# Chunked attention with two mixtures of experts, one core: v in rows interleaved by head, k copied by POOL, k and q in one transfer

## The chip, the core and the metric

The kernel runs as one program on one core of one Trainium2 chip. The core has five engines with an instruction queue each: PE (matrix multiply, with PEld for its weight loads), DVE and ACT (elementwise work and reductions), POOL (the same) and SP, which here issues the transfers between HBM and SBUF. Sixteen DMA engines carry the transfers out. SBUF has 128 partitions (rows). The metric is the device time of one execution in microseconds; three runs of the kernel before took 248.13, 250.2 and 254.1 us, the median is 250.2.

## What is computed

Attention in chunks of 32 queries: each chunk sees 8 memory rows, 16 rows to its left, its own 32 and 8 to its right. A soft mixture of experts and then a top-1 mixture follow on the 3072 tokens of 512 features.

```python
q, k, v: (4, 8, 768, 64);  mem_k, mem_v: (4, 8, 8, 64)
for c in range(24):
    k_ctx = k[:, :, max(0, 32*c - 16) : min(768, 32*c + 40)]      # v_ctx likewise
    k_full = concatenate([mem_k, k_ctx]);  v_full = concatenate([mem_v, v_ctx])
    s = q_c @ k_full.T / 8
    a = exp(s - max(s));  a = a / (sum(a) + 1e-9)
    out[:, :, 32*c : 32*c + 32] = a @ v_full
x = out as (3072, 512)
logits = x @ phi                                # 8 experts with 4 slots each
slots = softmax(logits over tokens).T @ x       # (32, 512)
slot_out[e] = relu(slots[e] @ w1[e]) @ w2[e]    # 8 experts, w1 and w2 16.8 MB each
x = softmax(logits over slots) @ slot_out
y = top-1 mixture of x: gate, 8 experts, output gate
```

## The kernel before

**Tiles.** The attention stage goes over 24 tiles of 128 queries (`QT`), six to a batch entry (`TPB`); a tile has four chunks (`CPT`) of 32 (`CH`). The eight heads are kept in four pairs (`HP`), and the two heads of a pair are called r = 0 and 1. For q and k, partitions 0 to 63 hold the 64 features of head 0 of each pair, 64 to 127 those of head 1. A chunk's window in `k` is 64 columns for each of both heads of a pair: 32 of the chunk before and after (its halo), fresh ones and 8 memory ones; `k` has zeros where r and the partition half do not match, so that one matmul gives both heads' scores. `v` is laid out the other way: partitions hold the window's 64 positions, 0 to 63 for head 0 and 64 to 127 for head 1. Of these 64, the first 24 (`PREV`) are the halo, the next 8 (`NMEM`) memory and the last 32 the chunk's own block; the free dimension holds r, chunk, pair and feature, again with zeros off the diagonal.

**Loads.** SP issues all loads, in program order: `load_ks` and `load_q` (256 KB each, three buffers), and `load_v`, which for each r loads the 32 fresh rows of four chunks (128 KB, `vd`), and for the first tile of a batch entry the 32 halo and memory rows (`vpd`), for the next two the 8 memory rows (`vmd`; three `v` buffers then keep them). An SP instruction that waits holds up all those behind it. `load_w` brings the weights of the first mixture, 32 tiles of 1 MB: 14 go to a ring of buffers (`NRING`) during the attention stage, spread evenly over its iterations by `want`; six more (`mid`) go into the space that the attention buffers leave, and the rest follow as ring tiles come free.

**Copies.** `expand_k` builds `k` (two buffers) for a tile: for each r the fresh rows by ACT (line 180), then the halo from the tile before and, for the first two tiles of a batch entry, the memory rows by POOL (lines 185 and 187, through `copy_pool`). `shift_v` fills v's halo for every tile but a batch entry's first: for each r two copies on POOL, one from the same tile's fresh rows and one from the tile before, across partitions.

**Order.** The order is written by hand. Iteration `it` does `scores(it)`, `softmax_b(it - 1)`, `logit_a(it - 4)`, `ptrans(it - 1)`, `expand_k(it + 1)` (two ahead in the first iterations, by the table `EARLY`), `shift_v(it - 1)`, `softmax_a(it)`, `pv(it - 2)` and `xtrans(it - 3)`; SP's `load_qk(it + 3)` stands behind the scores and `load_v(it + 1)` behind pv. Every fourth iteration adds the slot sums of a group of four tiles (`group_d`). `softmax_a` takes a maximum, subtracts it in three pieces that bring the window's columns into v's order, and ACT takes the exponential; `softmax_b` sums. After the stage come the slots, the eight experts (`ffn1`, `ffn_t`, `ffn2`), and the second mixture, none of which the change touches.

Of the kernel before, what the change touches and what calls it, by code (L numbers as in the profile page):

```python
# [9 lines left out]
F32 = mybir.dt.float32  # L10
# [4 lines left out]
ALU = mybir.AluOpType  # L15
AX = mybir.AxisListType
# [54 lines left out]
def attention_soft_moe_top1_moe(  # L71
    ctx: ExitStack,
    tc: tile.TileContext,
    qd: bass.AP,
    kd: bass.AP,
    kpd: bass.AP,
    kmd: bass.AP,
    vd: bass.AP,
    vpd: bass.AP,
    vmd: bass.AP,  # L80
    phid: bass.AP,
    w1d: bass.AP,
    w2d: bass.AP,
    wgd: bass.AP,
    v1d: bass.AP,
# [36 lines left out]
    ones = const.tile([128, 128], F32, name="ones")  # L122
    phi = const.tile([128, KD, NS], F32, name="phi")
    wg = const.tile([128, KD, 2 * E], F32, name="wg")
    lall = const.tile([128, QT, NS], F32, name="lall")
# [28 lines left out]
    def v_view(i):  # L154
        return v_t[i % 3].rearrange("p (r c h d) -> p r c h d", r=2, c=CPT, h=HP)

    def load_ks(i):
        ks_t[i] = ap.tile([128, HP, CPT, CH], F32, tag="ks", name="ks", bufs=3)
        nc.sync.dma_start(out=ks_t[i], in_=kd[i])

    def load_q(i):
        q_t[i] = ap.tile([128, HP, 128], F32, tag="q", name="q", bufs=3)
        nc.sync.dma_start(out=q_t[i], in_=qd[i])

    def load_qk(i):
        load_ks(i)
        load_q(i)

    def copy_pool(out, in_):
        nc.gpsimd.tensor_scalar(out=out, in0=in_, scalar1=1.0, scalar2=0.0, op0=ALU.mult, op1=ALU.add)  # L170

    def expand_k(i, first=False):
        b, t = divmod(i, TPB)
        k, ks = k_view(i), ks_t[i]
        kb = k[:, :, :, PREV:].rearrange("p r h (j c) -> p r h j c", j=CPT)
        for r in range(2):
            p = slice(64 * r, 64 * r + 64)
            eng = nc.vector.tensor_copy if first and r else nc.scalar.copy
            copy = nc.vector.tensor_copy if first and r else copy_pool
            eng(out=kb[p, r, :, :, NMEM:], in_=ks[p])  # L180
            if t == 0:
                prev = kprev[p, b]
            else:
                prev = k_view(i - 1)[p, r, :, KCOLS - PREV:]
            copy(out=k[p, r, :, 0:PREV], in_=prev)
            if t < 2:
                copy(
                    out=kb[p, r, :, :, 0:NMEM],
                    in_=kmem[p, b].unsqueeze(2).to_broadcast([64, HP, CPT, NMEM]),
                )  # L190
# [12 lines left out]
    def shift_v(i):  # L203
        if i % TPB == 0:
            return
        v = v_view(i)
        for r in range(2):
            p0 = 64 * r
            copy_pool(v[p0:p0 + PREV, r, 1:], v[p0 + 32:p0 + 32 + PREV, r, 0:CPT - 1])
            copy_pool(v[p0:p0 + PREV, r, 0], v_view(i - 1)[p0 + 32:p0 + 32 + PREV, r, CPT - 1])  # L210

# [47 lines left out]
    def softmax_a(i):  # L259
        s3 = st.pop(("sc", i)).rearrange("p (h c) -> p h c", h=H)  # L260
        if i % TPB == 0:
            nc.vector.memset(s3[0:32, :, 0:LEFT], NEG)
        if i % TPB == TPB - 1:
            nc.vector.memset(s3[96:128, :, KW - RIGHT:KW], NEG)
        mx = small.tile([128, H], F32, tag="mx", name="mx")
        nc.vector.tensor_reduce(out=mx, in_=s3, axis=AX.X, op=ALU.max)  # L266
        sub = work.tile([128, H, KW], F32, tag="sub", name="sub", bufs=3)
        for dst, src, n in ((0, 0, 32), (32, 40, PREV), (32 + PREV, 32, FRESH)):
            nc.vector.tensor_tensor(  # L269
                out=sub[:, :, dst:dst + n], in0=s3[:, :, src:src + n],  # L270
                in1=mx.unsqueeze(2).to_broadcast([128, H, n]), op=ALU.subtract,
            )
        p = sub.rearrange("p h c -> p (h c)")
        nc.scalar.activation(out=p, in_=p, func=ACTF.Exp, scale=SCALE)  # L274
        st["p", i] = p

    def softmax_b(i):
        p = st["p", i]
        sm = small.tile([128, H], F32, tag="sm", name="sm", bufs=4)
        nc.vector.tensor_reduce(  # L280
            out=sm, in_=p.rearrange("p (h c) -> p h c", h=H), axis=AX.X, op=ALU.add
        )
        nc.vector.tensor_scalar(out=sm, in0=sm, scalar1=EPS, scalar2=None, op0=ALU.add)
        nc.vector.reciprocal(out=sm, in_=sm)
        st["r", i] = sm
# [620 lines left out]
    with tc.manual_schedule():  # L906
        load_ks(0)
        kprev = ap.tile([128, B, HP, PREV], F32, name="kprev")
        kmem = ap.tile([128, B, HP, NMEM], F32, name="kmem")
        nc.sync.dma_start(out=kprev, in_=kpd)  # L910
        nc.sync.dma_start(out=kmem, in_=kmd)
        load_q(0)
# [679 lines left out]
def _layout(inputs):  # L1592
# [34 lines left out]
    return {
        "qd": qh,
        "kd": kw,
        "kpd": kp,  # L1630
        "kmd": km,
        "vd": vb,
        "vpd": np.ascontiguousarray(vp),
        "vmd": np.ascontiguousarray(vm),
        "phid": np.ascontiguousarray(inputs["moe_phi"]),
        "w1d": np.ascontiguousarray(inputs["moe_w1"]),
        "w2d": np.ascontiguousarray(inputs["moe_w2"]),
        "wgd": np.ascontiguousarray(wg),
        "v1d": np.ascontiguousarray(inputs["moe2_w1"]),
# [20 lines left out]
```

## Time and profile before

| | us |
|---|---|
| three runs, median | 250.2 |
| the profiled execution | 251.28 |
| its span, first to last instruction | 249.7 |
| busy in the span: PE | 213.5 |
| DVE | 155.0 |
| ACT | 125.3 |
| POOL | 96.6 |

The span has four parts: the attention stage up to the last `pv` (130.2 us), the slots (to 139.75 us, where the first expert matmul starts), the experts of the first mixture (to 182 us) and the second mixture. The granted TensorE clock is 0.956 on the mean of the span. The busy share of the 16 DMA engines can read slightly above 1; the amount moved stands beside it in GB/s. A wait is the idle time of an engine ahead of an instruction, put down to what ended it.

### The profile page before, as it was taken

The numbers are of one execution on the slowest core, as the hardware profiler recorded it, in microseconds if no ns is written. First come the engines' busy times: TensorE is split into PE (matmuls) and PEld (weight loads), VectorE is DVE, ScalarE is ACT, GpSimd is POOL, SyncE is SP. The second block draws the span as 40 slices with busy tenths as digits, with TensorE's granted clock in tenths as the row PEclk, the third lists the DMA queues.
The fourth block names the chain that finished last, engine by engine and source line by source line (L and its number), as shares of the span: only waits on it lengthen the run. The fifth ranks groups of instructions, "written<-read, shape, count | busy, mean of one in ns | idle before, by whom it ended". The sixth has DMA issues, their size and how long they took to land.

```text
span 249.7 us, 7344 instructions
## 1 busy us (share of the span) xinstructions
PE 213.5 (86%) x2826; PEld 147.7 (59%) x2826; DVE 155.0 (62%) x454; ACT 125.3 (50%) x256; POOL 96.6 (39%) x235
## 2 busy tenths in 40 slices
PE   6785997999697788858779999999999999999960
PEld 5573775766475565635566343345468847878850
DVE  4897578778766787865865367154125579774430
ACT  3465385667565765655633224242245355437840
POOL 4678461476424674345740012281002453121000
PEclk9998699999999999999999999999999569999996
DMA  6979999989999898997999799999691110743450
GB/s 193 301 192 321 338 253 312 308 295 326 232 331 306 243 367 241 308 304 228 352 389 405 241 371 403 408 406 383 240 403 47 42 43 1 286 168 149 186 225 9
DMA packets 34376, 65.91 MB, mean 264 GB/s; under 512 B 3744, under 2 KB 5280, under 8 KB 34336
## 3 DMA queue, kind: packets, MB, share of 16 engines
q1 hardware_dynamic: 34176, 64.86, 77.7%
q0 software_dynamic: 160, 0.52, 0.8%
q8 instruction: 24, 0.39, 0.7%
q14 instruction: 16, 0.13, 0.2%
HBM read 59.08 MB, written 6.29 MB: 262 GB/s over the span
## 4 chain that ended last, share of the span: by engine, by line
PE 51%; DMA 28%; ACT 6%; POOL 5%; issue 3%; DVE 2%; SPq 2%; POOLq 0%; ACTq 0%; DVEq 0%
DMA v<-vd 11%; DMA ks<-kd 11%; PE g L1508 10%; PE sc L504 6%; PE pv L537 6%; POOL v L170 4%; PE tp L521 3%; DMA ring<-w1d 3%; DMA q<-qd 3%; PE pv L302 2%; PE sc L250 2%; ACT k L180 2%; PE tp L291 2%; PE mi L332 2%; PE g L1366 1%
## 5 line engine op out<-in xcount | busy, mean ns | idle before, releaser
L170 POOL TENSOR_SCALAR v<-v 24x768 f32<-24x768 f32 x80 | 49.2, 616 | 43.9 <-DMA v<-vd 38.9
L180 ACT COPY k<-ks 64x512 f32<-64x512 f32 x47 | 28.9, 614 | 19.4 <-DMA ks<-kd 17.6
L250 PE MATMUL sc<-k,q 128*32 128x128 f32 x768 | 27.4, 286 | 11.1 <-ACT k L180 7.2
L302 PE MATMUL pv<-v,pt 128*32 128x128 f32 x768 | 27.4, 282 | 7.6 <-POOL v L170 5.1
L250 PEld LDWEIGHTS sc<-k,q 128*32 128x32 f32 x768 | 21.2, 114 | 15.9 <-issue 11.0
L1508 PE MATMUL g<-ring,ring 128*128 128x512 f32 (+1 forms) x125 | 30.6, 388 | 0.0
L302 PEld LDWEIGHTS pv<-v,pt 128*32 128x32 f32 x768 | 20.2, 112 | 12.6 <-POOL v L170 7.3
L1508 PEld LDWEIGHTS g<-ring,ring 128*128 128x128 f32 x125 | 22.6, 188 | 6.4 <-issue 1.3
L280 DVE TENSOR_REDUCE sm<-sub 128x8 f32<-128x512 f32 x24 | 16.4, 682 | 12.8 <-ACT sub L274 12.7
L311 DVE TENSOR_TENSOR x<-pv,sm 128x512 f32<-128x512 f32 x24 | 16.5, 685 | 9.9 <-PE pv L302 9.7
L293 ACT ACTIVATE pt<-tp 128x512 f32<-128x512 f32 x24 | 14.2, 597 | 14.0 <-PE tp L291 14.0
L269 DVE TENSOR_TENSOR sub<-sc,mx 128x256 f32<-128x256 f32 (+2 forms) x72 | 19.7, 329 | 0.8
L509 ACT ACTIVATE hs<-sc 128x512 f32<-128x512 f32 x16 | 9.6, 597 | 21.2 <-PE sc L504 20.3
L266 DVE TENSOR_REDUCE mx<-sc 128x8 f32<-128x512 f32 x24 | 16.1, 670 | 0.3
L291 PE MATMUL tp<-ident,sub 128*128 128x128 f32 x96 | 15.9, 292 | 0.0
L1523 DVE TENSOR_SCALAR ring<-g,scl 128x512 f32<-128x512 f32 (+1 forms) x12 | 8.6, 726 | 11.5 <-PE g L1508 11.5
L274 ACT ACTIVATE sub<-sub 128x512 f32<-128x512 f32 x24 | 15.0, 630 | 1.4 <-DVE sub L269 0.9
L332 PE MATMUL mi<-xt,phi 128*32 128x128 f32 x176 | 9.8, 289 | 5.9 <-ACT xt L325 3.8
L323 PE MATMUL tp<-ident,x 128*128 128x128 f32 x88 | 14.5, 288 | 0.1
L170 POOL TENSOR_SCALAR k<-k 64x96 f32<-64x96 f32 x40 | 10.9, 272 | 8.7 <-ACT k L180 3.4
L325 ACT ACTIVATE xt<-tp 128x512 f32<-128x512 f32 x22 | 12.8, 584 | 2.5 <-PE tp L323 2.5
L537 PE MATMUL pv<-ring,hz 128*32 128x512 f32 x112 | 13.4, 596 | 0.6 <-DVE hz L527 0.6
(324 smaller groups left out, 370.2 us busy)
## 6 DMA issues: line engine op xcount, KB each, us to landing
ring<-w2d SPq DMA_DIRECT2D x14, 1024.0 KB
ring<-w1d SPq DMA_DIRECT2D x12, 1024.0 KB
ks<-kd SPq DMA_DIRECT2D x24, 256.0 KB
q<-qd SPq DMA_DIRECT2D x24, 256.0 KB
v<-vd SPq DMA_DIRECT2D x48, 128.0 KB
out<-ring SPq DMA_DIRECT2D x10, 512.0 KB
mid<-w1d SPq DMA_DIRECT2D x4, 1024.0 KB
mid<-w2d SPq DMA_DIRECT2D x2, 1024.0 KB
```

The source lines that it names most:

```text
L170: nc.gpsimd.tensor_scalar(out=out, in0=in_, scalar1=1.0, scalar2=0.0, op0=ALU.mult, op1=ALU.add)
L180: eng(out=kb[p, r, :, :, NMEM:], in_=ks[p])
L250: nc.tensor.matmul(out=sc[32 * j:32 * j + 32, 128 * h:128 * h + 128], lhsT=q[:, h, 32 * j:32 * j + 32], rhs=k[:, :, h, KBLK * j:KBLK * j + ...
L266: nc.vector.tensor_reduce(out=mx, in_=s3, axis=AX.X, op=ALU.max)
L269: nc.vector.tensor_tensor(out=sub[:, :, dst:dst + n], in0=s3[:, :, src:src + n], in1=mx.unsqueeze(2).to_broadcast([128, H, n]), op=ALU.sub ...
L274: nc.scalar.activation(out=p, in_=p, func=ACTF.Exp, scale=SCALE)
L280: nc.vector.tensor_reduce(out=sm, in_=p.rearrange("p (h c) -> p h c", h=H), axis=AX.X, op=ALU.add)
L291: nc.tensor.transpose(tp[:, 128 * h:128 * h + 128], p[:, 128 * h:128 * h + 128], ident)
L302: nc.tensor.matmul(out=po[32 * j:32 * j + 32, 128 * h:128 * h + 128], lhsT=pt[:, 128 * h + 32 * j:128 * h + 32 * j + 32], rhs=v[:, :, j, h ...
L311: nc.vector.tensor_tensor(out=x.rearrange("p (h d) -> p h d", h=H), in0=po.rearrange("p (h d) -> p h d", h=H), in1=r.unsqueeze(2).to_broad ...
L537: nc.tensor.matmul(out=so[32 * j:32 * j + 32, :], lhsT=hz[:, k, :], rhs=w[k // 4][:, j, :], start=(e == 0 and k < 4), stop=(e == E - 1 and ...
L1508: nc.tensor.matmul(out=ps[t][:, q], lhsT=h[:, x, ts], rhs=wq[:, y, q], start=(n == 0), stop=(n == 4), skip_group_check=True,)
```

## The change

*v.* The host lays v out with halo and memory rows in place: for each tile and r one array of 64 positions by 1024 (chunk, pair, feature), 256 KB. In SBUF position s of head r stands in partition 2s + r, so each of the two transfers per tile writes every second partition of all 128. `shift_v` and the transfers of `vpd` and `vmd` go. The buffers are zeroed whole beforehand, so the loads of the first three tiles wait for these memsets, which stand on POOL (buffers 0 and 2) and DVE (buffer 1). To match, `softmax_a` writes its difference as (pair, column, r), in one instruction instead of three, and `softmax_b` sums over it with that stride.

*k and q.* One transfer of 512 KB for a tile brings both (for tile 0 two, as before). From tile 4 on POOL copies k's fresh rows instead of ACT. The halo of a batch entry's first tile and its memory rows come as one small tile per entry (`kpm`, 64 KB, two buffers) in place of two loads for all four at the start.

*Weights.* `phi` and the gates are one load. The ring tiles are due earlier: one is issued among the first loads, ahead of v 1, two in iteration 2, the other eleven spread over the rest.

```diff
-    def load_ks(i):
-        ks_t[i] = ap.tile([128, HP, CPT, CH], F32, tag="ks", name="ks", bufs=3)
-        nc.sync.dma_start(out=ks_t[i], in_=kd[i])
-
-    def load_q(i):
-        q_t[i] = ap.tile([128, HP, 128], F32, tag="q", name="q", bufs=3)
-        nc.sync.dma_start(out=q_t[i], in_=qd[i])
+    def load_kpm(b):
+        kpm[b] = ap.tile([128, HP, PREV + NMEM], F32, tag="kpm", name="kpm", bufs=2)
+        nc.sync.dma_start(out=kpm[b], in_=kpmd[b])
 
     def load_qk(i):
-        load_ks(i)
-        load_q(i)
+        t = ap.tile([128, 2, HP * CPT * CH], F32, tag="kq", name="kq", bufs=3)
+        ks_t[i] = t[:, 0].rearrange("p (h j c) -> p h j c", h=HP, j=CPT)
+        q_t[i] = t[:, 1].rearrange("p (h t) -> p h t", h=HP)
+        if i == 0:
+            nc.sync.dma_start(out=t[:, 0], in_=kqd[i, :, 0])
+            load_kpm(0)
+            nc.sync.dma_start(out=t[:, 1], in_=kqd[i, :, 1])
+        else:
+            nc.sync.dma_start(out=t, in_=kqd[i])
...
-            eng = nc.vector.tensor_copy if first and r else nc.scalar.copy
+            eng = nc.vector.tensor_copy if first and r else nc.scalar.copy if i < 4 else copy_pool
...
     def load_v(i):
-        v = v_view(i)
-        b, t = divmod(i, TPB)
+        v = v_t[i % 3].rearrange("(s r) f -> s r f", r=2)
         for r in range(2):
-            p0 = 64 * r
-            nc.sync.dma_start(out=v[p0 + 32:p0 + 64, r], in_=vd[i, r])
-            if t == 0:
-                nc.sync.dma_start(out=v[p0:p0 + 32, r], in_=vpd[b, r])
-            elif t < 3:
-                nc.sync.dma_start(out=v[p0 + PREV:p0 + 32, r], in_=vmd[b, r])
-
-    def shift_v(i):
...
+            nc.sync.dma_start(out=v[:, r, VCOLS * r:VCOLS * r + VCOLS], in_=vd[i, r])
...
-        sub = work.tile([128, H, KW], F32, tag="sub", name="sub", bufs=3)
-        for dst, src, n in ((0, 0, 32), (32, 40, PREV), (32 + PREV, 32, FRESH)):
-            nc.vector.tensor_tensor(
-                out=sub[:, :, dst:dst + n], in0=s3[:, :, src:src + n],
-                in1=mx.unsqueeze(2).to_broadcast([128, H, n]), op=ALU.subtract,
-            )
-        p = sub.rearrange("p h c -> p (h c)")
+        sub = work.tile([128, HP, KW, 2], F32, tag="sub", name="sub", bufs=3)
+        nc.vector.tensor_tensor(
+            out=sub.rearrange("p h c r -> p h r c"), in0=s3.rearrange("p (h r) c -> p h r c", r=2),
+            in1=mx.rearrange("p (h r) -> p h r", r=2).unsqueeze(3).to_broadcast([128, HP, 2, KW]),
+            op=ALU.subtract,
+        )
+        p = sub.rearrange("p h c r -> p (h c r)")
...
-            out=sm, in_=p.rearrange("p (h c) -> p h c", h=H), axis=AX.X, op=ALU.add
+            out=sm.rearrange("p (h r) -> p h r", r=2),
+            in_=p.rearrange("p (h c r) -> p h r c", h=HP, r=2), axis=AX.X, op=ALU.add,
...
-                want = (it - 1) * NRING / (QT - 3)
+                want = 2 + (it - 1) * (NRING - 2) / (QT - 3)
```

What stands in a row on the engines, first on POOL in the middle of the stage. A row names the line, the operation, what it writes and reads, and the shape; `x2` is two alike in a row. Before, the shifts of tile 8, the halo of k for tile 11 and the shifts of tile 9 (the `v` buffers are 120 to 122, the `k` buffers 118 and 119):

```order
L170 TENSOR_SCALAR v_122<-v_122 24x768
L170 TENSOR_SCALAR v_122<-v_121 24x256
L170 TENSOR_SCALAR v_122<-v_122 24x768
L170 TENSOR_SCALAR v_122<-v_121 24x256
L170 TENSOR_SCALAR k_119<-k_118 64x4x24 x2
L170 TENSOR_SCALAR v_120<-v_120 24x768
L170 TENSOR_SCALAR v_120<-v_122 24x256
L170 TENSOR_SCALAR v_120<-v_120 24x768
L170 TENSOR_SCALAR v_120<-v_122 24x256
```

Now, tiles 10 and 11 of k (buffers 114 and 115; `kq` is the loaded tile):

```order
L168 TENSOR_SCALAR k_114<-kq 64x4x4x32
L168 TENSOR_SCALAR k_114<-k_115 64x4x24
L168 TENSOR_SCALAR k_114<-kq 64x4x4x32
L168 TENSOR_SCALAR k_114<-k_115 64x4x24
L168 TENSOR_SCALAR k_115<-kq 64x4x4x32
L168 TENSOR_SCALAR k_115<-k_114 64x4x24
L168 TENSOR_SCALAR k_115<-kq 64x4x4x32
L168 TENSOR_SCALAR k_115<-k_114 64x4x24
```

Nothing on POOL waits for v any more in this stage; the whole expansion of k is on it, in the order of the tiles.

SP at the start of the program, before:

```order
L159 DMA ks<-kd 128x512
L910 DMA kprev<-kpd 128x384
L911 DMA kmem<-kmd 128x128
L163 DMA q<-qd 128x512
L159 DMA ks<-kd 128x512
L163 DMA q<-qd 128x512
L197 DMA v_120<-vd 32x1024
L199 DMA v_120<-vpd 32x1024
L197 DMA v_120<-vd 32x1024
L199 DMA v_120<-vpd 32x1024
L159 DMA ks<-kd 128x512
L163 DMA q<-qd 128x512
```

And now:

```order
L161 DMA kq<-kqd 128x512
L154 DMA kpm<-kpmd 128x128
L163 DMA kq<-kqd 128x512
L165 DMA kq<-kqd 128x1024
L193 DMA v_116<-vd 64x1024 x2
L165 DMA kq<-kqd 128x1024
L209 DMA ring_126<-w1d 128x4x512
L193 DMA v_117<-vd 64x1024 x2
L921 DMA pg<-pgd 128x192
L154 DMA kpm<-kpmd 128x128
L165 DMA kq<-kqd 128x1024
L193 DMA v_118<-vd 64x1024 x2
```

The first ring tile now stands among the first loads, between kq of tile 2 and v of tile 1 (buffer 117).

SP at the end of the stage, before:

```order
L159 DMA ks<-kd 128x512
L163 DMA q<-qd 128x512
L197 DMA v_120<-vd 32x1024 x2
L231 DMA ring_1979<-w2d 128x4x512
L197 DMA v_121<-vd 32x1024 x2
L231 DMA ring_2078<-w2d 128x4x512
L197 DMA v_122<-vd 32x1024 x2
L226 DMA mid_2334<-w1d 128x4x512
```

And now:

```order
L165 DMA kq<-kqd 128x1024
L193 DMA v_116<-vd 64x1024 x2
L193 DMA v_117<-vd 64x1024 x2
L214 DMA ring_1894<-w2d 128x4x512
L193 DMA v_118<-vd 64x1024 x2
L209 DMA mid_2134<-w1d 128x4x512
```

The last v stands behind the last ring tile in both.

## Rows read from the trace of the kernel before

**Rows 1.** Page, chain that ended last: shares of the span by line.

```profile
DMA v<-vd 11%; DMA ks<-kd 11%; PE g L1508 10%; PE sc L504 6%; PE pv L537 6%; POOL v L170 4%; PE tp L521 3%; DMA ring<-w1d 3%; DMA q<-qd 3%; PE pv L302 2%; PE sc L250 2%; ACT k L180 2%; PE tp L291 2%; PE mi L332 2%; PE g L1366 1%
```

**Rows 2.** Stretches: length; busy us (count): PE, PEld, DVE, ACT, POOL; clock, DMA, GB/s.

```profile
0.00:126.30 126.30, 101.03 (x1971) 75.25 (x1974) 92.14 (x258) 74.28 (x142) 69.63 (x150) 0.97 0.94 288
...
139.70:182.00 42.30, 41.65 (x360) 17.98 (x360) 18.31 (x66) 13.32 (x28) 10.04 (x60) 1.00 0.93 348
```

**Rows 3.** The same view of narrow stretches.

```profile
22.50:25.50 3.00, 2.04 (x20) 1.31 (x24) 2.44 (x7) 1.43 (x4) 2.72 (x6) 0.57 1.05 399
26.00:27.50 1.50, 1.50 (x23) 1.08 (x16) 0.41 (x1) 0.37 (x1) 0.41 (x2) 0.50 1.05 225
...
41.50:43.00 1.50, 0.84 (x22) 0.38 (x13) 1.33 (x5) 0.51 (x2) 0.00 (x0) 1.00 0.98 217
...
128.00:138.00 10.00, 9.26 (x136) 6.31 (x134) 6.79 (x26) 3.86 (x12) 1.57 (x4) 1.00 1.05 407
```

**Rows 4.** Timeline, SP and POOL: start, us, instruction [idle before, what ended it].

```profile
21.06 1.70 SPq L197 DMA_DIRECT2D v<-vd  x2
...
29.37 2.66 POOL L170 TENSOR_SCALAR v<-v 24x768 f32<-24x768 f32 x4 [2.88 <-DMA v<-vd]
...
37.89 0.33 SPq L197 DMA_DIRECT2D v<-vd  x1
...
45.41 2.70 POOL L170 TENSOR_SCALAR v<-v 24x768 f32<-24x768 f32 x4 [4.19 <-DMA v<-vd]
```

**Rows 5.** Page, groups: line, engine, operation, count; busy us, mean ns; idle before, releaser.

```profile
L170 POOL TENSOR_SCALAR v<-v 24x768 f32<-24x768 f32 x80 | 49.2, 616 | 43.9 <-DMA v<-vd 38.9
L180 ACT COPY k<-ks 64x512 f32<-64x512 f32 x47 | 28.9, 614 | 19.4 <-DMA ks<-kd 17.6
...
L311 DVE TENSOR_TENSOR x<-pv,sm 128x512 f32<-128x512 f32 x24 | 16.5, 685 | 9.9 <-PE pv L302 9.7
```

**Rows 6.** Waits: who waited for whom, us in total, times, longest.

```profile
PE sc L250 <- ACT k L180: 7.2, 6, 2.2
...
PE pv L302 <- POOL v L170: 5.1, 8, 1.2
```

**Rows 7.** DMA issues: what, count and KB of each.

```profile
ks<-kd SPq DMA_DIRECT2D x24, 256.0 KB
...
v<-vd SPq DMA_DIRECT2D x48, 128.0 KB
...
v<-vpd SPq DMA_DIRECT2D x8, 128.0 KB
...
v<-vmd SPq DMA_DIRECT2D x16, 32.0 KB
```

**Rows 8.** Chain that ended last, in order of time: start, us, what.

```profile
120.01 6.26 DMA v<-vd
...
129.12 1.12 PE pv L302 x32
```

**Rows 9.** Timeline, PE: scores of tiles 4, 10, 11, 12 and 23.

```profile
19.56 1.08 PE L250 MATMUL sc<-k,q 128*32 128x128 f32 x32
...
51.06 1.08 PE L250 MATMUL sc<-k,q 128*32 128x128 f32 x32
...
56.06 1.08 PE L250 MATMUL sc<-k,q 128*32 128x128 f32 x32
...
60.11 1.08 PE L250 MATMUL sc<-k,q 128*32 128x128 f32 x32
...
120.02 1.08 PE L250 MATMUL sc<-k,q 128*32 128x128 f32 x32
```

**Rows 10.** Instructions by form: count, ns min/median/max, first and last start, forms.

```profile
L170 POOL TENSOR_SCALAR v<-v x80: 397/630/869, 15.2 to 128.7; 24x768 f32<-24x768 f32 x40, 24x256 f32<-24x256 f32 x40
L170 POOL TENSOR_SCALAR k<-k x40: 266/271/347, 5.8 to 118.3; 64x96 f32<-64x96 f32 x40
...
L925 POOL MEMSET v<- x2: 945/946/946, 9.0 to 12.4; 64x1024 f32 x2
```

More of the change, by code (lines that the diff above doesn't have):

```diff
@@ L122, in attention_soft_moe_top1_moe @@
     ones = const.tile([128, 128], F32, name="ones")
-    phi = const.tile([128, KD, NS], F32, name="phi")
-    wg = const.tile([128, KD, 2 * E], F32, name="wg")
+    pg = const.tile([128, KD, NS + 2 * E], F32, name="pg")
+    phi, wg = pg[:, :, 0:NS], pg[:, :, NS:]
     lall = const.tile([128, QT, NS], F32, name="lall")
@@ L181, in expand_k @@
             if t == 0:
-                prev = kprev[p, b]
+                prev = kpm[b][p, :, 0:PREV]
             else:
@@ L188, in expand_k @@
                     out=kb[p, r, :, :, 0:NMEM],
-                    in_=kmem[p, b].unsqueeze(2).to_broadcast([64, HP, CPT, NMEM]),
+                    in_=kpm[b][p, :, PREV:].unsqueeze(2).to_broadcast([64, HP, CPT, NMEM]),
                 )
     def load_v(i):
-        v = v_view(i)
-        b, t = divmod(i, TPB)
+        v = v_t[i % 3].rearrange("(s r) f -> s r f", r=2)
         for r in range(2):
-            p0 = 64 * r
-            nc.sync.dma_start(out=v[p0 + 32:p0 + 64, r], in_=vd[i, r])
-            if t == 0:
-                nc.sync.dma_start(out=v[p0:p0 + 32, r], in_=vpd[b, r])
-            elif t < 3:
-                nc.sync.dma_start(out=v[p0 + PREV:p0 + 32, r], in_=vmd[b, r])
-    def shift_v(i):
[L204 to L210, printed above, removed]
+            nc.sync.dma_start(out=v[:, r, VCOLS * r:VCOLS * r + VCOLS], in_=vd[i, r])
     order = [(1, 0, 0), (1, 0, 1)]
@@ L906, in attention_soft_moe_top1_moe @@
     with tc.manual_schedule():
[L907 to L912, printed above, removed]
+        load_qk(0)
         for i in range(2):
@@ L917, in attention_soft_moe_top1_moe @@
         load_qk(1)
+        nc.gpsimd.memset(v_t[0], 0.0)
         load_v(0)
         load_qk(2)
-        load_v(1)
-        load_qk(3)
-        load_v(2)
+        load_w()
         def zero_off(eng, t):
@@ L939, in attention_soft_moe_top1_moe @@
         expand_k(0, first=True)
-        zero_off(nc.vector, v_view(0))
+        nc.vector.memset(v_t[1], 0.0)
+        nc.gpsimd.memset(v_t[2], 0.0)
+        load_v(1)
+        nc.sync.dma_start(out=pg, in_=pgd)
+        load_kpm(1)
+        load_qk(3)
+        load_v(2)
         nc.vector.tensor_reduce(
@@ L954, in attention_soft_moe_top1_moe @@
                 load_qk(it + 3)
-            if it == 0:
-                nc.sync.dma_start(out=phi, in_=phid.rearrange("(k p) s -> p k s", p=128))
-                nc.sync.dma_start(out=wg, in_=wgd.rearrange("(k p) s -> p k s", p=128))
+            if it % TPB == 3 and it // TPB + 2 < B:
+                load_kpm(it // TPB + 2)
             if it < len(WAKE) - 1:
@@ L1626, in _layout, with rows @@
-    wg = np.concatenate([inputs["moe2_w_gate"], inputs["moe2_w_output_gate"]], axis=1)
+    va[:, :, :, PREV:32] = vm[:, None, :, :, None]
+    def rows(a):
+        return a.reshape(KD, 128, a.shape[1]).transpose(1, 0, 2)
+    pg = np.concatenate([inputs["moe_phi"], inputs["moe2_w_gate"], inputs["moe2_w_output_gate"]], axis=1)
     return {
[L1628 to L1635, printed above, removed]
+        "kqd": np.ascontiguousarray(np.stack([kw, qh], axis=2)),
+        "kpmd": np.ascontiguousarray(np.concatenate([kp, km], axis=3)),
+        "vd": va.reshape(QT, 2, 64, CPT * HP * D),
+        "pgd": np.ascontiguousarray(rows(pg)),
```

43 lines of the change are left out of this document (13 added, 30 removed).

## The prediction

> **What bounds the kernel now.** First the chain of work that ended last [rows 1]: among its lines the loads of v and of k come first, with 11% of the span each. Both belong to the attention stage, so the next view is the busy time by stretch [rows 2]. From 0 to 126.3 us the 16 DMA engines are busy 0.94 of the time, while PE is busy 101.0 of 126.3 us; in the expert stage (139.7 to 182 us) PE is busy 41.65 of 42.3 us and nothing is to be had there. So the attention stage is where the change can act, and DMA is its limit.
>
> The third view is narrow stretches [rows 3]. Where weights dominate, the engines move 399 to 407 GB/s at a busy share of 1.05. In the stretches at 26 us and at 41.5 us they are as busy (1.05 and 0.98) and move 225 and 217 GB/s. What is in flight there is v: SP issued it at 21.06 and at 37.89 us, and POOL's next shift waited until 29.37 and 45.41 us for it [rows 4]. An engine that is busy and moves half is not short of work; something about the v transfer is slow, and its neighbours in the queue slow down with it.
>
> The fourth view is the large groups of instructions [rows 5]. POOL spends 49.2 us on the shifts of v and idles 38.9 us for the load of v ahead of them; ACT idles 17.6 us for k. PE waits directly for little of this, 7.2 us for the k copies and 5.1 us for the shifts [rows 6], because most of its delay is queued behind those waits.
>
> **How slow v is.** Full rate per unit of busy share is 407/1.05 = 388 GB/s [rows 3]. Over 0 to 126.3 us: 0.94 x 126.3 = 118.7 us busy, 288 GB/s x 126.3 us = 36.4 MB [rows 2], which at 388 is 93.8 us. The excess is 24.9 us. v's own bytes, 48 x 128 KB, 8 x 128 KB and 16 x 32 KB [rows 7], are 7.86 MB, 20.3 us at full rate. If v pays the whole excess, it costs 45.2 us, a rate of 174 GB/s.
>
> **The change, part by part.** *Bytes.* Until the last v: kq 24 x 512 KB (ks of [rows 7] and as much for q), v 48 x 256 KB (64 rows of 4 KB instead of 32), the small loads 0.36 MB, and 14 ring tiles of 1 MB: 40.2 MB, of which v 12.58 MB. That is 4.7 MB more for v than before, 12 us of DMA at full rate; this term speaks against the change. *Rate of v.* Before, one transfer writes 32 neighbouring partitions; after, one writes 64 rows, every second partition of all 128. The trace has no transfer of that shape. Its two bounds are 174 GB/s (v as it is) and 388 (the stretches of weights, which write 128 partitions). I take 388, because the new transfer resembles those in the partitions it spans, and the halved stretches are those of a transfer that sits in a quarter of the partitions.
>
> [...]
>
> *Sum.* 40.2 MB at 388 is 103.7 us of share; at the share of 0.94 that DMA holds in this stage [rows 2], the last v lands at 110.4 us. Before, it landed at 120.01 + 6.26 = 126.3 us, and the last pv ended at 129.12 + 1.12 = 130.2 us [rows 8], after four shifts on POOL (2.7 us [rows 4]). Without them it ends 1.1 us after v, at 111.5 us. *PE's floor.* An undisturbed iteration takes 4.05 us from scores to scores, and 5.0 us where the group's slot sums stand in it [rows 9]; from the scores of tile 4 at 19.56 us, 15 x 4.05 + 4 x 5.0 = 80.8 us bring those of tile 23 to 100.3 us. Before, they began at 120.02 us [rows 9], and the last pv ended 10.2 us later: 110.5 us. So two limits lie 1% apart.
>
> *k on POOL.* 40 copies of 64x512 leave ACT (614 ns each [rows 5], 24.6 us) and go to POOL. A copy of that size is not in POOL's trace; between its 256 and 768 elements, 397 and 869 ns [rows 10], I take 630. Per tile POOL then does 2 x 0.63 + 2 x 0.27 = 1.8 us instead of 4 x 0.616 + 2 x 0.27 = 3.0 us [rows 5, 10], and cannot bind. The chain from k's landing to the scores grows from 2 x 0.614 + 0.27 = 1.5 us to 1.8 us, and k now lands together with q, half a transfer later (256 KB at 407 GB/s: 0.65 us). While loads land ahead, the preceding iteration's PE work covers this; uncovered it costs about 1 us each time. PE waited for the k copies 6 times [rows 6], so the bounds are 0 and 6 us; with the two limits so close that not every load lands ahead, I take 3 us. The last pv then ends at 114.5 us.
>
> *The rest, at nothing.* Zeroing whole v tiles takes as many columns as zeroing two halves did (0.95 us each [rows 10]). POOL's first one now stands ahead of the identity and of k's halo: its 1.9 us can show once, at the start, where the first scores also need q, and q comes 0.5 us earlier because the small loads ahead of it shrink by 192 KB. SP's load of v 0 waits for that memset, and kq 2 and the first ring tile queue behind it; they are wanted only in the iterations that follow. That ring tile, 2.7 us of DMA ahead of v 1 and kq 3, is one of the 14 already counted. On DVE one subtraction, at best as long as the product of that size (685 ns [rows 5]), replaces three; DVE is off the path. SP issues fewer transfers.
>
> *After the stage.* The 119.5 us from 130.2 to 249.7 stay if the weights keep up: 18 tiles remain, 18.9 MB, 49 us of share from 110.4 us on, so they are in by 163 us; the experts would end at 182 - 16 = 166 us. So 15.7 us come off. The profiled execution took 251.28 us for its span of 249.7, 0.4% above the median of 250.2: 251.28 - 15.7 = **236 us**.
>
> **Rivals.** *A, v gains only part.* The other 27.6 MB take 71.3 us of share. For the stage to end at 130.2 as before, v must land at 129.1: 0.94 x 129.1 - 71.3 = 50.1 us for 12.58 MB, 251 GB/s. From 230 to 277 GB/s the stage moves less than 5 us: no change, **about 251 us**. For it speaks that the excess may not be v's alone.
>
> *B, v stays as slow per byte.* [...] At 174 GB/s v takes 72.3 us, the last v lands at 143.6/0.94 = 152.7 us, the stage ends at 153.8 and the kernel at **275 us**; at 215 GB/s it is 260 us. Below 251 GB/s it costs time. For it: loads beside v are halved too [rows 3], so the partitions are not the only possible cause. Against it: the new rows reach every part of SBUF in one transfer, which the old ones did not. [...]
>
> *C, DVE becomes the bound.* The subtraction now writes, and the sum reads, every second element. Had both to double from 685 ns, DVE's 92.14/24 = 3.84 us per tile [rows 2] would grow by at most 1.0 us to 4.8, against 80.8/19 = 4.25 for PE: 20 x 0.6 = 12 us on the floor of 110.5, and the kernel at **244 us**. No row shows such an access. *D, hidden anyway.* PE busy 101.0 of 126.3 us leaves too much idle time for a freed DMA to show nothing.
>
> **How the numbers follow.** The forecast has 0.58, C 0.06, A 0.15, B 0.21, D nothing. About 2% is what a measurement of this kernel tells from no change (its runs lie between 248.13 and 254.1). Forecast and C are faster by over 2%: 0.64. A: 0.15. B: 0.21. The forecast's own range is 229 to 243: from a stage that ends before PE's floor, its tail shortened by POOL's 2.7 us (108), up to a v at 320 GB/s. The range for 8 in 10 runs from 229 to 260: it takes in A and the near third of B, and leaves out B's far end.
>
> **What would show it.** Right: stretches with v in flight move over 350 GB/s at a share of 1.05; from tile 4's scores to tile 23's it is 81 to 88 us; the last pv ends at 110 to 119 us; POOL's waits for v are gone and no wait for kq of that size replaces them. Wrong: stretches at 220 GB/s that last longer than now (B); iterations of 4.8 us with DVE full (C). The forecast fails above all if v's rate stays below 277 GB/s.

## The result, and the profile after

The changed kernel takes **236.75 us** in the median (235.19 to 241.22) against 250.18 beside it: a ratio of 0.947, 95% interval 0.938 to 0.956. Forecast were 236.0 us and a range of 229 to 260. The profiled execution took 236.62 us for a span of 234.9 (before: 251.28 and 249.7), so 14.8 us of span are to be explained. Medians are of all runs; the ratios to before, here and below, are of those runs alone that are not over 1.5% slower than the fastest of their kernel.

The same stretches as in [rows 2], of the kernel after: the attention stage up to the last `pv`, the slots, the experts, the second mixture (length; busy us of PE, PEld, DVE, ACT, POOL; clock, DMA share, GB/s).

```profile
0.00:118.10 118.10, 102.32 (x2033) 80.20 (x2037) 90.39 (x216) 53.95 (x105) 47.21 (x114) 0.94 0.95 356
118.10:128.50 10.40, 9.56 (x123) 6.13 (x117) 6.18 (x24) 2.87 (x10) 0.00 (x0) 1.00 1.03 380
128.50:170.00 41.50, 40.89 (x356) 17.69 (x348) 18.18 (x65) 13.31 (x28) 10.08 (x60) 1.00 0.97 368
170.00:234.90 64.90, 58.40 (x333) 45.18 (x329) 34.98 (x100) 33.18 (x73) 13.90 (x19) 0.91 0.38 144
```

The last `pv` ends at 118.1 us instead of 130.2. DMA is as busy as before (0.95), but moves 356 GB/s instead of 292 over the whole stage. The other 2.7 us lie behind the stage (116.8 us after the last `pv` instead of 119.5), and not in the change: from the last score matmul of the experts (173.8 us before, 161.66 after) to the span's end it is 75.9 us before and 73.2 after, and 73.3 in the kernel before with one part left out (e6 below); the traces of the other runs have 72.3 to 75.1. So the profiled execution of before had a long end.

Narrow stretches of the stage after, to set against [rows 3]; SP issued v at 9.92, 33.38 and 65.50 us.

```profile
10.00:15.00 5.00, 3.55 (x60) 2.93 (x50) 3.40 (x7) 2.38 (x4) 0.54 (x2) 0.63 1.05 410
15.00:20.00 5.00, 3.65 (x45) 3.12 (x47) 1.40 (x4) 2.95 (x5) 0.59 (x2) 0.50 0.72 289
20.00:25.00 5.00, 5.00 (x116) 3.94 (x108) 4.51 (x9) 1.83 (x3) 2.90 (x8) 0.84 0.59 202
...
35.00:40.00 5.00, 4.35 (x78) 3.44 (x79) 1.56 (x3) 1.26 (x3) 2.17 (x6) 0.66 1.03 414
...
65.00:70.00 5.00, 3.90 (x77) 2.79 (x73) 4.76 (x14) 2.12 (x6) 2.24 (x6) 1.00 1.04 416
```

With v in flight the engines now move 410 to 416 GB/s at a share of 1.03 to 1.05: the stretches that were busy and moved half are gone. New is the gap from 15 to 25 us, where DMA has too little to do (0.72 and 0.59). It is not the granted clock's, which is 0.50 from 15 to 20 us here: in the second trace of the changed kernel (e0 below) the clock is 1.00 over the first 25 us, and DMA's share of them is 0.81 (0.77 here). Its cause, in the timelines of ACT, PE and SP (start, us, instruction, idle before and what ended it):

```profile
16.23 1.26 ACT L178 COPY k<-kq 64x512 f32<-64x512 f32 x2 [3.14 <-DMA kq<-kqd]
...
17.52 1.09 ACT L277 ACTIVATE pt<-tp 128x512 f32<-128x512 f32 x2
18.16 1.48 PEld L286 LDWEIGHTS pv<-v,pt 128*32 128x32 f32 x32 [1.75 <-ACT pt L277]
...
20.16 1.12 SPq L193 DMA_DIRECT2D v<-vd  x2
...
21.33 1.13 SPq L209 DMA_DIRECT2D ring<-w1d  x2
```

ACT waits for kq of tile 3, the first `pt` stands behind that copy, the first `pv` behind `pt`, and SP can't issue v of tile 3 until that `pv` has freed its buffer (a wait of 5.7 us); the two ring tiles and kq of tile 6 stand behind it on SP. So tile 4's scores begin at 23.88 us (before: 19.56), and tile 6 waits for its k:

```profile
35.65 1.94 PE L233 MATMUL sc<-k,kq 128*32 128x128 f32 x32 [3.62 <-POOL k L168]
```

The chain that ended last, by line, to set against [rows 1]:

```profile
DMA kq<-kqd 16%; PE g L1486 10%; PE sc L488 6%; PE pv L521 6%; PE pv L286 6%; PE sc L233 6%; PE tp L505 3%; PE tp L275 3%; POOL k L168 3%; PE tp L307 2%; PE mi L330 2%; PE mi L316 2%; PE g L1362 1%; PE g L1344 1%; PE g L1328 1%
```

v and its shifts have left it; kq is first, with 16%, mostly ahead of POOL's copies. In order of time (start, us, what) the last load of the stage in it is this one:

```profile
55.44 8.55 DMA kq<-kqd
```

From 64.0 us to the last `pv` the chain goes over the engines alone, most of it on PE. (In e0's trace its last load of the stage, a kq, lands at 98.7 us.)

The groups of instructions that the change touched, by form (count | busy us, mean ns | idle before, releasers):

```profile
L168 POOL TENSOR_SCALAR k<-kq 64x512 f32<-64x512 f32 x40 | 24.7, 617 | 57.0 <-DMA kq<-kqd 44.4 <-PE mi L316 4.5 <-PE sc L233 3.8
...
L263 DVE TENSOR_REDUCE sm<-sub 128x8 f32<-128x512 f32 x24 | 17.0, 708 | 0.6 <-ACT sub L257 0.6
L251 DVE TENSOR_TENSOR sub<-sc,mx 128x512 f32<-128x512 f32 x24 | 16.8, 698 | 0.8
```

POOL's copy of k takes 617 ns (ACT's took 614). The strided subtraction (698 ns) and the strided sum (708 ns) cost little more than contiguous ones: in e1 below, where both are contiguous, they take 692 and 676 ns.

### The profile page after: what moved, and what is told of

It reads as the page before. It is cut to its first block, busy times and chain, and to the rows that moved or that the text cites. A ratio compares the mean times of both kernels' runs of the same rounds, so it can differ in the third digit from the quotient of the medians.

```text
span 234.9 us, 7045 instructions
## 1 busy us (share of the span) xinstructions
PE 211.2 (90%) x2826; PEld 149.2 (64%) x2826; DVE 149.7 (64%) x405; ACT 103.3 (44%) x216; POOL 71.2 (30%) x193
## 3 DMA queue, kind: packets, MB, share of 16 engines
q1 hardware_dynamic: 31136, 69.57, 78.7%
## 4 chain that ended last, share of the span: by engine, by line
PE 65%; DMA 16%; DVE 7%; POOL 3%; issue 3%; ACT 3%; SPq 2%; POOLq 0%; ACTq 0%; DVEq 0%
DMA kq<-kqd 16%; PE g L1486 10%; PE sc L488 6%; PE pv L521 6%; PE pv L286 6%; PE sc L233 6%; PE tp L505 3%; PE tp L275 3%; POOL k L168 3%; PE tp L307 2%; PE mi L330 2%; PE mi L316 2%; PE g L1362 1%; PE g L1344 1%; PE g L1328 1%
## 5 line engine op out<-in xcount | busy, mean ns | idle before, releaser
L168 POOL TENSOR_SCALAR k<-kq 64x512 f32<-64x512 f32 x40 | 24.7, 617 | 57.0 <-DMA kq<-kqd 44.4
L233 PE MATMUL sc<-k,kq 128*32 128x128 f32 x768 | 29.2, 294 | 11.0 <-POOL k L168 4.9
L233 PEld LDWEIGHTS sc<-k,kq 128*32 128x32 f32 x768 | 21.8, 117 | 15.8 <-POOL k L168 11.3
L263 DVE TENSOR_REDUCE sm<-sub 128x8 f32<-128x512 f32 x24 | 17.0, 708 | 0.6 <-ACT sub L257 0.6
L251 DVE TENSOR_TENSOR sub<-sc,mx 128x512 f32<-128x512 f32 x24 | 16.8, 698 | 0.8
L275 PE MATMUL tp<-ident,sub 128*128 128x128 f32 x96 | 16.6, 302 | 0.2 <-ACT sub L257 0.2
L324 ACT ACTIVATE ls<-mi 128x128 f32<-128x128 f32 x22 | 6.1, 277 | 19.3 <-PE mi L316 19.3
L307 PE MATMUL tp<-ident,x 128*128 128x128 f32 x88 | 14.0, 281 | 0.3 <-PE mi L330 0.2
L275 PEld LDWEIGHTS tp<-ident,sub 128*128 128x128 f32 x96 | 11.2, 151 | 4.2 <-PE sc L233 2.4
```

The source lines that it names most:

```text
L233: nc.tensor.matmul(out=sc[32 * j:32 * j + 32, 128 * h:128 * h + 128], lhsT=q[:, h, 32 * j:32 * j + 32], rhs=k[:, :, h, KBLK * j:KBLK * j + ...
L251: nc.vector.tensor_tensor(out=sub.rearrange("p h c r -> p h r c"), in0=s3.rearrange("p (h r) c -> p h r c", r=2), in1=mx.rearrange("p (h r ...
L263: nc.vector.tensor_reduce(out=sm.rearrange("p (h r) -> p h r", r=2), in_=p.rearrange("p (h c r) -> p h r c", h=HP, r=2), axis=AX.X, op=ALU ...
L275: nc.tensor.transpose(tp[:, 128 * h:128 * h + 128], p[:, 128 * h:128 * h + 128], ident)
L307: nc.tensor.transpose(tp[:, 128 * c:128 * c + 128], x[:, 128 * c:128 * c + 128], ident)
```

## The experiments

Two theories on the main gain: P, the partitions that a v transfer spans set DMA's rate; S, the gain is the shifts and the waits for them. "The changed kernel beside it" is e0_after_again, which ran with e2 to e4.

**e1_neighbours.** The changed kernel, v in neighbouring partitions.

```diff
-        v = v_t[i % 3].rearrange("(s r) f -> s r f", r=2)
+        v = v_t[i % 3]
         for r in range(2):
-            nc.sync.dma_start(out=v[:, r, VCOLS * r:VCOLS * r + VCOLS], in_=vd[i, r])
+            nc.sync.dma_start(out=v[64 * r:64 * r + 64, VCOLS * r:VCOLS * r + VCOLS], in_=vd[i, r])
```

(The difference and the sum are contiguous again, to match.)

> The changed kernel with one thing undone: each transfer of v writes its 64 rows of 4 KB into 64 neighbouring partitions (head 0 in 0 to 63, head 1 in 64 to 127) instead of every second one of 128. Bytes, number of transfers, halo rows in place and the absence of shifts stay. Theory P (the partitions that a transfer spans set its rate): v falls to the 217 to 225 GB/s of the old stretches; 12.6 MB then take 57 us of share instead of 32, the stage ends near 138 us instead of 118.1, and the kernel at 252 to 260 us. Theory S (the gain came from the shifts and the waits for them): nothing is lost, 235 to 239 us.

Measured: 283.75 us (278.54 to 291.0). By stretch:

```profile
0.00:158.10 158.10, 113.63 (x2032) 88.20 (x2036) 90.17 (x216) 53.29 (x105) 46.97 (x114) 0.87 0.99 267
40.00:140.00 100.00, 72.87 (x1317) 54.72 (x1305) 56.99 (x143) 31.85 (x67) 30.27 (x73) 0.86 1.04 262
```

For 100 us DMA is full and moves 262 GB/s; the stage ends at 158.1 us. P holds, and its price was set too low: 0.99 x 158.1 = 156.5 us busy for 267 x 158.1 = 42.2 MB, which at 388 GB/s are 108.8. Charged to v's 12.58 MB (32.4 us), the excess of 47.7 gives v 157 GB/s (an estimate). That is rival B of the prediction: the same bytes without the interleaving cost 47 us more, and 31 us more than the kernel before beside it.

So 64 neighbouring partitions did no better than 32: 157 GB/s for v here and 174 in the kernel before, both estimates of the same kind.

**e5_before_spread, e5b_before_spread.** The kernel before, its 32 rows into every fourth partition.

```diff
-            nc.sync.dma_start(out=v[p0 + 32:p0 + 64, r], in_=vd[i, r])
+            u = v_t[i % 3].rearrange("(s u) (r f) -> s u r f", u=4, r=2)
+            fresh, halo = (v[p0 + 32:p0 + 64, r], v[p0:p0 + 32, r]) if i < 3 else (u[:, 2 * r, r], u[:, 2 * r + 1, r])
+            nc.sync.dma_start(out=fresh, in_=vd[i, r] if i < 3 else vd[i, r].rearrange("p c h d -> p (c h d)"))
             if t == 0:
-                nc.sync.dma_start(out=v[p0:p0 + 32, r], in_=vpd[b, r])
-            elif t < 3:
+                nc.sync.dma_start(out=halo, in_=vpd[b, r] if i < 3 else vpd[b, r].rearrange("p c h d -> p (c h d)"))
+            elif t < 3 and i < 3:                 # e5b alone
...
-        with tc.If(others > 0):
+        with tc.If(others > NT + FF):             # e5b alone
```

> The kernel before with one thing done: from tile 3 on, the 32 rows of each v transfer go into every fourth of the 128 partitions instead of 32 neighbouring ones (as many bytes and transfers; shifts stay, the output is no longer the attention's). Theory P: the stretches at 217 to 225 GB/s go, the 24.9 us of excess DMA time shrink to a few, and the kernel takes 236 to 243 us although POOL still shifts. Theory S: the shifts still stand between v and pv, 247 to 251 us.

Measured: 1646.6 us, and neither theory meant that. The wrong outputs set off the second pass over all experts, and in the stage, which ended at 147.8 us, SP waited for v ahead of the small loads of memory rows that now overlap it. That wait of SP, and the stage:

```profile
SPq L203 <- DMA v<-vd: 42.1, 12, 6.5
```

```profile
0.00:147.80 147.80, 115.53 (x2032) 87.37 (x2036) 94.86 (x265) 76.36 (x145) 72.30 (x156) 0.90 0.76 259
```

A share of 0.76 and 259 GB/s is 341 GB/s per unit (before: 292 over 0.95, 307), but the time says nothing. So again, without both:

> The kernel before with the 32 rows of each v transfer in every fourth of 128 partitions from tile 3 on, without the confusion of e5_before_spread: from tile 3 on the small loads of memory rows are left out, since they overlap the spread rows and made SP wait for them, and so is the second pass over all experts at the end, which wrong outputs set off. Shifts stay; the output is not the attention's. Theory P (the partitions that a transfer spans set its rate): DMA moves over 320 GB/s through the stage, the last pv ends at 114 to 122 us instead of 130.2, the kernel takes 236 to 243 us. Theory S (the shifts and their waits held the stage): 247 to 251 us.

Measured: 237.04 us, ratio 0.947 (0.937 to 0.957).

```profile
0.00:118.00 118.00, 102.25 (x2033) 77.17 (x2037) 94.95 (x265) 75.54 (x145) 72.16 (x156) 0.99 0.93 317
```

P: with POOL's shifts in place (72 us busy, as before) and v's old bytes, less the 12 small loads (0.39 MB, about 1 us at 388 GB/s), spreading alone ends the stage at 118.0 us, where the whole change ends it in its first trace. Per unit of share DMA moves 317/0.93 = 341 GB/s, more than before (307) and less than after (375); what keeps it there was not tried.

**e6_before_no_shifts.** The kernel before; `shift_v` returns at once for tiles 3 to 23.

> The kernel before with the shifts of v on POOL left out from tile 3 on (the halo rows of v are then stale); the transfers of v stay as they are, 32 rows into 32 neighbouring partitions. Theory P: the DMA stretches at half rate stay and set the time; only the four shifts behind the last v and a little waiting go: 245 to 249 us. Theory S: the gain of the change is here, 235 to 241 us.

Measured: 250.07 us (248.56 to 251.23, just above P's 245 to 249) against 252.34 beside it; the last `pv` ends at 128.4 us.

```profile
0.00:128.40 128.40, 106.91 (x2032) 80.87 (x2036) 92.08 (x265) 76.25 (x145) 28.25 (x84) 0.95 0.95 289
```

POOL falls from 72.7 to 28.3 us, DMA stays at 289 GB/s, and the stage gets 1.8 us shorter: S falls. The 38.9 us that POOL waited for v [rows 5] were a symptom.

**e7_half_v.** The changed kernel, half of v's columns loaded from tile 3 on.

> The changed kernel with v's transfers cut to half their columns from tile 3 on (64 rows of 2 KB instead of 4 KB, same partitions; the other half of v is stale). 5.5 MB less, 14 us of DMA share. If DMA still bounds the attention stage after the change: PE's floor takes over, the stage ends 4 to 8 us earlier, 228 to 232 us. If PE and the start bound it already: 235 to 237 us.

Measured: 233.16 us (231.9 to 234.26); the last `pv` ends at 113.3 us, 4.8 earlier (3.4 earlier than in e0's trace). The time lies between the two forecasts and within the runs of the changed kernel (231.39 to 241.22), so it tells nothing; by the traces loads still set part of the stage after the change, but 14 us of DMA share less bring only 3.4 to 4.8 us.

**e0, e2, e3, e4: the smaller parts.** e2_k_on_act undoes POOL's copies, e3_kq_apart the merged transfer, e4_ring_behind the place of the first ring tile.

```diff
-            eng = nc.vector.tensor_copy if first and r else nc.scalar.copy if i < 4 else copy_pool
+            eng = nc.vector.tensor_copy if first and r else nc.scalar.copy                       # e2
...
-            nc.sync.dma_start(out=t, in_=kqd[i])
+            nc.sync.dma_start(out=t[:, 0], in_=kqd[i, :, 0])                                     # e3
+            nc.sync.dma_start(out=t[:, 1], in_=kqd[i, :, 1])
...
-        load_w()                                  # e4: from behind load_qk(2) ...
         load_v(1)
...
         load_v(2)
+        load_w()                                  # ... to here
```

> The changed kernel once more, as the measure for the three runs beside it: 235 to 238 us, the last pv at 118 us.

> The changed kernel with one thing undone: ACT copies k's fresh rows for all tiles, as before, and POOL only the halo. Theory K (POOL's copy costs what the prediction put on it): PE's 4.9 us of waiting for POOL's k fall, and the kernel gets 1 to 3 us faster than the changed one beside it. Rival Q (what is waited for is the load, and whoever copies waits for it): PE waits as long, for ACT's k instead; and since the transposed weights (pt), the exponentials and xt stand behind the waiting copy on ACT, the kernel gets 1 to 5 us slower.

> The changed kernel with one thing undone: k and q of every tile in two transfers of 256 KB, k first. Theory M (merging makes k land later): k lands 0.65 us earlier in each of the 4 to 5 places where PE waits for it, 1 to 3 us faster. Rival I: 22 more transfers for SP to issue, which use the earlier landing up, as do the loads behind them: within 1 us either way.

> The changed kernel with one thing moved: the first ring tile (1 MB) is issued behind v of tile 2 instead of ahead of v of tile 1. Theory L (the prediction's 'at nothing' for that tile is wrong): kq of tile 3, whose copy holds the first pt on ACT until 17.5 us, lands about 2.5 us earlier; the first pv and the loads behind it follow, tile 4's scores begin at 20 to 22 us instead of 23.9, and the kernel takes 2 to 4 us less. Rival N: the stage moves the same bytes in any order and DMA sets its end: within 1 us.

| | median, us | ratio to before (95%) |
|---|---|---|
| e0_after_again | 235.27 | 0.924 (0.915 to 0.932) |
| e2_k_on_act | 239.02 | 0.948 (0.942 to 0.955) |
| e3_kq_apart | 235.7 | 0.937 (0.930 to 0.943) |
| e4_ring_behind | 234.06 | 0.926 (0.919 to 0.933) |

The unchanged e0 has 0.924 here and had 0.947 in the first comparison, so kernels that ran apart are told apart no better than 2%. Beside each other, e2 alone is clear: 3.7 us slower than e0 by the medians, 2.6% by the ratios. The time is as rival Q had it, and of its reason the part on `xt` holds: `xt` stands behind the copies on ACT, whether they wait for a load or not. PE's timeline in e2, from scores to scores in an iteration without a stall:

```profile
40.33 1.08 PE L233 MATMUL sc<-k,kq 128*32 128x128 f32 x32 [0.17 <-issue]
41.42 0.43 PE L316 MATMUL mi<-xt,pg 128*32 128x128 f32 x8
...
44.37 1.08 PE L233 MATMUL sc<-k,kq 128*32 128x128 f32 x32
```

And the same in the kernel after:

```profile
40.86 1.08 PE L233 MATMUL sc<-k,kq 128*32 128x128 f32 x32
41.76 0.40 PE L316 MATMUL mi<-xt,pg 128*32 128x128 f32 x8
...
44.50 1.08 PE L233 MATMUL sc<-k,kq 128*32 128x128 f32 x32
```

4.04 us against 3.64, and 4.05 before [rows 9]. With k on ACT, ACT is busy 63.58 of the 96 us from 20 to 116 us (44.18 after), and PE's weight loads of `mi` wait for ACT's `xt` 17 times (6.6 us; after: 6 times, 2.5 us). The same weight loads in the two iterations above, e2 first, then the kernel after, where they wait for nothing:

```profile
41.42 0.16 PEld L316 LDWEIGHTS mi<-xt,pg 128*32 128x32 f32 x8 [0.28 <-ACT xt L309]
...
41.65 0.24 PEld L316 LDWEIGHTS mi<-xt,pg 128*32 128x32 f32 x8
```

`mi` starts 1.09 us behind the scores in e2 and 0.90 after, 0.19 of the 0.40 us; most of the rest lies ahead of the next scores, whose weight loads wait 0.33 us for POOL's halo of k in e2. So it is the pace that POOL's copies improve, in many iterations, and no single wait.

e3: 0.4 us slower by the medians and 1.4% by the ratios; M, by which it would be faster, falls, and a small loss can't be told from nothing. e4: in its trace ACT's copies of tile 3's k start at 14.66 us instead of 16.23 and tile 4's scores at 22.29 instead of 23.88, but e0's trace has 22.54 without the move, and the ratios (0.926 and 0.924) and 1.2 us in the median can't be told from nothing (N). That was the tile that the prediction put at nothing.

**e8, e9, e10: the gap at the start.** e9_two_ahead moves two ring tiles ahead of v of tile 3, e8_ring_ahead the ring tiles of all iterations from behind `load_v` to behind `load_qk`, e10_both_moves adds e4's move.

```diff
             if 3 < it + 3 < QT:
                 load_qk(it + 3)
+            if it >= 2:
+                want = 2 + (it - 1) * (NRING - 2) / (QT - 3)
+                while nload[0] < min(want, NRING):
+                    load_w()
```

(The same lines are gone behind `load_v(it + 1)`.)

> The changed kernel with one thing moved: the two ring tiles of iteration 2 are issued ahead of v of tile 3, for whose buffer SP waits until about 20 us, instead of behind it. Theory G (the gap of 15 to 25 us, where the DMA share is 0.72 and 0.59, is lost for good, since DMA sets the stage's end): the gap closes by 2 to 3 us of share, kq of tile 6 comes earlier, and the stage and the kernel end 2 to 3 us sooner, 232 to 234 us. Rival O (the order of loads only moves the stall, as with the first ring tile): within 1 us.

> The changed kernel with every ring tile of the stage issued behind kq and ahead of v, for whose buffer SP waits 33.6 us in all, instead of behind v. Theory G: DMA's other gaps (share 0.91 at 45 us, 0.93 and 0.89 at 100 to 110 us) close as well, 3 to 5 us off, 231 to 233 us. Rival O: v lands 2.7 us later behind each ring tile, PE waits for v in its place, and the time is within 1 us or longer.

> e8_ring_ahead and e4_ring_behind together: the ring tiles of the stage ahead of v, and the very first one behind v of tile 2. In e8_ring_ahead tile 4's scores start at 24.06 us and those of tile 23 78.9 us later, which is PE's pace without a stall (80.8 us by the rows of before), while DMA falls to a share of 0.60 near the end. Theory F (PE's floor now sets the stage, so its start counts in full): the earlier kq of tile 3, which bought nothing in e4_ring_behind while DMA set the end, brings tile 4's scores to about 22.2 us and the last pv from 110.3 to 108.4 us; 227 to 229.5 us. Rival D (DMA still sets the end): last pv at 110 us or later, 230 to 232 us.

e8 takes **230.73 us** (six runs, 229.83 to 231.57; ratio 0.922, 0.916 to 0.928). Of the eleven runs of the changed kernel ten are above 231.57. e9 takes 233.23 us (229.36 to 238.35; ratio 0.931, 0.924 to 0.938; in the profiled execution, its fastest, the last `pv` ends at 110.8 us), e10 231.37 us (230.08 to 237.18; 0.924, 0.918 to 0.930). The stage of e8:

```profile
0.00:25.00 25.00, 18.50 (x268) 15.51 (x272) 15.87 (x30) 10.26 (x16) 11.83 (x28) 0.86 0.93 350
25.00:110.26 85.26, 82.57 (x1776) 63.51 (x1768) 73.93 (x186) 43.76 (x89) 35.22 (x86) 1.00 1.00 390
```

The same of the kernel after:

```profile
0.00:25.00 25.00, 18.09 (x272) 15.35 (x272) 16.06 (x31) 10.29 (x16) 11.87 (x28) 0.80 0.77 281
25.00:118.10 93.10, 84.23 (x1769) 64.84 (x1765) 74.33 (x185) 43.66 (x89) 35.35 (x86) 0.98 1.00 376
```

In the first 25 us e8 moves 350 GB/s instead of 281; the difference, 69 x 25 = 1.7 MB, is 4.6 us at 376 GB/s (an estimate). Later it moves 390 instead of 376, and the last `pv` ends at 110.3 us. By the traces G holds for the gap: it was lost for good. The time shows it less firmly: the median is 4.5 us below e0's (235.27), but the ratios, 0.922 and 0.924, are not told apart, and e9 is not told from e0 either. No wait of PE for v appears among its waits, though the ring tiles now go ahead of v. e10 shows the other side: tile 4's scores come at 22.55 us instead of 24.06, but DMA moves only 316 GB/s in the first 25 us, tiles 4 to 23 take 82.3 us instead of 78.9, and the stage ends at 112.1. In this pair the early ring tile is what fills DMA at the start; F falls, though the times of e8 and e10 can't be told apart.

**What sets the stage now.** Scores of tiles 6 and 23, in e5b, the kernel after and e8:

```profile
29.33 1.08 PE L252 MATMUL sc<-k,q 128*32 128x128 f32 x32
110.44 1.08 PE L252 MATMUL sc<-k,q 128*32 128x128 f32 x32
...
35.65 1.94 PE L233 MATMUL sc<-k,kq 128*32 128x128 f32 x32 [3.62 <-POOL k L168]
110.70 1.08 PE L233 MATMUL sc<-k,kq 128*32 128x128 f32 x32
...
31.33 1.08 PE L233 MATMUL sc<-k,kq 128*32 128x128 f32 x32
102.97 1.08 PE L233 MATMUL sc<-k,kq 128*32 128x128 f32 x32
```

| us | tile 6's scores at | tile 6 to tile 23 | last `pv` ends |
|---|---|---|---|
| before | 32.87 | 87.2 | 130.2 |
| e5b_before_spread | 29.33 | 81.1 | 118.0 |
| after | 35.65 | 75.1 | 118.1 |
| e0_after_again | 36.47 | 73.0 | 116.7 |
| e2_k_on_act | 35.07 | 78.7 | 121.1 |
| e7_half_v | 33.71 | 72.3 | 113.3 |
| e8_ring_ahead | 31.33 | 71.6 | 110.3 |

So e5b and the kernel after end the stage at the same time by different ways: the rest of the change makes the middle about 6 us shorter, and its later start takes those 6 us back. And from tile 6 on, with half of v's bytes or with the loads in a better order, the middle takes 71.6 to 72.3 us, 0.6 to 3.4 us less than in the two traces of the changed kernel: by these traces what is left there is mostly the engines' own pace.

## Why the prediction was right, and where not

**The cause and the rate: right.** v at the full rate was the step on which all hung. Excess DMA time in the stage: 0.95 x 118.1 = 112.2 us busy for 356 x 118.1 = 42.0 MB, 108.4 us at 388: 3.8 us, where 24.9 stood before. e1 and e5b show it from both sides. POOL's shifts were rightly taken for victims (e6), and "what would show it" came: over 400 GB/s with v in flight, 86.8 us from tile 4's scores to tile 23's (81 to 88 forecast), the last `pv` at 118.1 (110 to 119). One of these signs failed in part: POOL's waits for v are gone, but waits for kq of that size did replace them (44.4 us). Three of them stand in the chain that ended last, the last behind the load of 55.44 us; the others do not.

**The sum: right to 0.9 us of span, with two errors against each other.** The stage ends at 118.1 us instead of 114.5 (+3.6), what follows is 116.8 us instead of 119.5 (-2.7). The second is the long end of the profiled execution of before, which the sum took over; it is scatter, not insight. And the 3 us that the sum put on POOL's copies, which cost nothing (below), filled in for the late start, which it put at nothing: that the total fits is luck in part. The path to the end was another one, too: not the last v and a `pv` right behind it (PE waits 0.2 us for v in the whole stage), but the last scores at 110.70 us and the softmax behind them, 7.4 us.

**"The rest, at nothing": wrong.** The prediction saw that kq and a ring tile queue behind v on SP, and called it harmless. The step that failed is this one: the share of 0.94 kept from before held on the mean (0.95), but the first 25 us got 0.77 at 281 GB/s, because v of tile 3 waits for the first `pv` and the ring tiles wait behind v. Tile 6's scores start at 35.65 us, where e5b has 29.33. The traces of e8 and after put an estimated 4.6 us on it.

**PE's floor of 110.5 us: about right, with two errors against each other.** The 4.05 us of an undisturbed iteration were PE's pace with ACT's copies in the way (in the trace of before, too, `mi` waits 0.28 us for `xt`, at 57.15 us); without, the shortest take 3.64 us. But more of them are long than the four with the slot sums: in e8, 8 of the 19 from tile 4 to tile 23 take 3.6 to 3.9 us and 11 take 4.2 to 4.7, together 78.9 instead of 80.8. So the two limits do lie close together, as the prediction had it, only that they take turns: loads hold the chain up to 64.0 us in the trace after (98.7 in e0's), the engines behind it. That e8's stage ends at 110.3 us, so near that floor, is chance: its parts are others (tile 4 at 24.06 instead of 19.56, then 78.9 instead of 80.8, then 7.3 instead of 10.2).

**k on POOL, +3 us: wrong in sign.** POOL's copy was estimated rightly (630 ns, measured 617), and the chain from load to scores did get longer; but e2 shows the move worth about 3.7 us, since it takes 40 copies off ACT, and PE's weight loads then wait less for ACT's `xt` (2.5 us instead of e2's 6.6).

**The rivals.** C: the strided accesses cost next to nothing (698 and 708 ns, 692 and 676 contiguous in e1); the one subtraction replaces three of 425, 348 and 215 ns, 0.29 us less per tile. A: it would have needed v below 277 GB/s; with the excess of 3.8 us v has 12.58 MB in 32.4 + 3.8 us, 347 GB/s. B is what would have come without the interleaving (e1), and worse than its 275 us.

## What to carry to other kernels

Where DMA is busy and moves half (225 GB/s at a share of 1.05, against 407 [rows 3]), look at which partitions the transfer in flight writes; spreading the same rows over all 128 was worth most of the gain here (e5b has a ratio of 0.947; the change had 0.947 and 0.924), and placing them badly cost 47 us (e1). An engine's long waits next to it are symptoms until a run without the waiting work says otherwise (e6: 44.4 us less work on POOL, a stage 1.8 us shorter). When a load must wait for its buffer, let loads that need none go ahead of it on the queue (e8: 350 GB/s instead of 281 in the first 25 us, less clear in the time), and read an engine's pace from an iteration in which it waits for nobody, not from the shortest one seen (3.64 us here, where 4.05 was taken).

## What the runs showed of the hardware that was not expected

Sixty-four neighbouring partitions were no better than 32: an estimated 157 GB/s for v in e1 and 174 before, from the excess of DMA time in both. DMA moved 262 GB/s in all over 100 us of e1, at a share of 1.04, and the median kq landed 13.0 us after its issue (7.7 in the kernel after). With v in every fourth of 128 partitions (e5b, from tile 3 on) DMA moved 341 GB/s per unit of share, with v in every second (after) 375, in the kernel before 307. And the access with a stride of two elements on DVE, both written and read, took 698 and 708 ns for 128x512, 1 and 5% longer than the contiguous ones of e1 (692 and 676 ns).
